# A looped general path behind the main code, a split first exponential and a separate last tile, in an attention kernel

## The chip, the core and the metric

The kernel runs on one core of a Trainium2 chip. The metric is device time in microseconds (us) of one execution. The profile describes one execution each. Engines are PE (TensorE, matmuls; PEld its weight loads), ACT (ScalarE, here the exponentials), DVE (VectorE), POOL (GpSimd) and SP (SyncE, here issuing most transfers); "PEq" and the like are their sequencers.

## The reference

```python
B, Hq, Hkv, Sq, Sk, D = 16, 32, 8, 288, 512, 128       # bf16
k = jnp.repeat(k, Hq // Hkv, axis=1); v = jnp.repeat(v, Hq // Hkv, axis=1)
scores = jnp.einsum("bhqd,bhkd->bhqk", q, k) * D ** -0.5
out = jnp.einsum("bhqk,bhkd->bhqd", softmax(scores), v)
```

There are 16 x 8 = 128 groups (one key/value head with its four query heads: 1152 query rows, nine tiles of 128). The kernel leaves out the subtraction of the row maximum. Every row sum of exponentials is checked against a range; if one falls outside, a **general path** at the end computes everything again with the maximum. With the inputs given it never runs, but its code is part of the program.

## The kernel before

A group is three chunks of 1536 score columns (NC = 3, 384 chunks in all). For each chunk PE makes six score matmuls (`op_s`), ACT one exponential (`op_exp`), PE twelve matmuls with the values (`op_pv`, two chunks later, LAG = 2), DVE a reciprocal and a scaling. Where the general path stands, and how the end chooses it:

```python
def general(eng, key, after):                # called in each engine's head
    home[key] = nc.cur_bb
    br = eng.br(after + key)                 # jump over the general path ...
    if key in hints:
        br.branch_hint(hints[key])           # ... hinted at an earlier place
    with nc.body("general_" + key):
        ...
        fns[key](eng)                        # its unrolled code
        eng.br("done_" + key)
    nc.switch_bb(after + key)

def choose(eng, key, behind=False):          # at each engine's end
    eng.wait_ge(sem["s_flag"], 1)
    reg = eng.alloc_register("bad_" + key)
    eng.load(reg, flag_i[:])
    ...
    br = eng.br_ne(reg, 0, "general_" + key, "done_" + key)
    ...                                      # PE alone has its general path here
```

The heads of ACT, PE and SP:

```python
@block.scalar
def _(eng):
    op_kd(eng, 0)                            # load of key group 0, 128 KB
    ...
    emit(eng, [("s_one", 1)], lambda: eng.activation(dum[:, 1:2], dum[:, 0:1], ACTF.Exp))
    op_kc(eng, 0, range(NJ // 2, NJ), 1, 2)  # copy of half the transposed keys
    op_kd(eng, 1)                            # key group 1, 128 KB
    op_v(0, eng, 0, 2)                       # values of groups 0 and 1, 256 KB
    general(eng, "act", "main_")
    for n in range(NS):
        op_exp(n)
    op_ev_act()                              # scales the very last query tile
    choose(eng, "act")

@block.tensor
def _(eng):
    for x in range(WARM): ...                # 5 matmuls of zeros, 512 columns
    op_kt(0, range(half), 0)                 # key transposes
    op_kt(0, range(half, NJ), 1)
    for n in range(NS):
        if n == LAG:
            op_kt(1, range(NJ), 1)
        ...
        op_s(n)
        if n >= LAG:
            op_pv(n - LAG)
    ...

first = [lambda i=i: op_q0(i) for i in range(NC)]   # SP: query group 0 in 3 parts
first += [lambda: op_q(1), lambda: op_k(0, 2), lambda: op_q(2), ...]
```

Of the kernel before, what the change touches and what calls it, by code (L numbers as in the profile page):

```python
# [16 lines left out]
def general_path(nc, es, q, k, v, out, s_go):  # L17

    B, Hq, Sq, D = q.shape
    _, Hkv, Sk, _ = k.shape  # L20
    rep = Hq // Hkv
    P = 128
    NJ = Sk // P
    NT = (rep * Sq) // P
    G = Hkv
    NG = B * G
    U = NG * NT
    UPB = G * NT
    FREE = NJ * P
    scale = float(D) ** -0.5  # L30
    DV = D + 1
    OPB = 3
    NSB, NXB, NS, NX, NPB, NM, NR, XPB = 3, 3, 3, 4, 4, 8, 2, 2
    LAG_XT, LAG_PV = 3.0, 8.0
    n_xc = U // XPB
    n_oc = U // OPB

    q_v = q.rearrange("b h s d -> b (h s) d")
    k_v = k.rearrange("b g s d -> b (g s) d")
    o_v = out.rearrange("b h s d -> b (h s) d").rearrange("b (c p) d -> b p c d", p=P)  # L40
    v_v = v.rearrange("b g s d -> b (g s) d").rearrange("b (c p) d -> b p c d", p=P)

    v_sb = es.enter_context(nc.sbuf_tensor("gv_sb", [P, 2, G, NJ, DV], BF16))
    o_sb = es.enter_context(nc.sbuf_tensor("go_sb", [P, 2, G, NT, D], BF16))
    qt_sb = es.enter_context(nc.sbuf_tensor("gqt_sb", [P, 2, G, NT, P], BF16))
    kt_sb = es.enter_context(nc.sbuf_tensor("gkt_sb", [P, 2, G, NJ, P], BF16))
    sn_sb = es.enter_context(nc.sbuf_tensor("gsn_sb", [P, NS, FREE], FP32))
    x_sb = es.enter_context(nc.sbuf_tensor("gx_sb", [P, NX, FREE], BF16))
    pt_sb = es.enter_context(nc.sbuf_tensor("gpt_sb", [P, NPB, XPB, NJ, P], BF16))
    nmx_sb = es.enter_context(nc.sbuf_tensor("gnmx_sb", [P, NM], FP32))  # L50
    rl_sb = es.enter_context(nc.sbuf_tensor("grl_sb", [P, NR, OPB], FP32))
    ident = es.enter_context(nc.sbuf_tensor("gident", [P, P], BF16))
    ones_sb = es.enter_context(nc.sbuf_tensor("gones_sb", [P, P], BF16))
    ps_s = es.enter_context(nc.psum_tensor("gps_s", [P, NSB, FREE], FP32))
    ps_x = es.enter_context(nc.psum_tensor("gps_x", [P, NXB, XPB, NJ, P], BF16))
    ps_o = es.enter_context(nc.psum_tensor("gps_o", [P, 2, 512], FP32))

    class Chan:
        def __init__(self, name, n):
            self.n = n  # L60
            self.sems = [es.enter_context(nc.semaphore("g_%s%d" % (name, i))) for i in range(n)]

        def w(self, i, mult=1):
            return (self.sems[i % self.n], (i // self.n + 1) * mult)

        def s(self, i):
            return self.sems[i % self.n]

    c_ldq = Chan("ldq", 2)
    c_ldk = Chan("ldk", 2)  # L70
    c_ldv = Chan("ldv", 2)
    c_out = Chan("outd", 2)
    c_s = Chan("s", NSB)
    c_dve = Chan("dve", NS)
    c_pool = Chan("pool", NX)
    c_xt = Chan("xt", NX)
    c_xc = Chan("xc", NXB)
    c_exp = Chan("exp", NPB)
    c_pv = Chan("pv", 7)
    c_rc = Chan("rc", NR)  # L80
    c_oev = Chan("oev", 2)
    s_init = es.enter_context(nc.semaphore("g_init"))
    s_c0 = es.enter_context(nc.semaphore("g_c0"))

    def emit(eng, waits, fn):
        for (s, n) in waits[:-1]:
            eng.wait_ge(s, n)
        ins = fn()
        if waits:
            s, n = waits[-1]  # L90
            ins.wait_op(s, n, "sem-ge")
        return ins

    def op_load(b):
        eng = nc.sync
        bb = b % 2
        if b >= 2:
            last = (b - 1) * UPB - 1
            eng.wait_ge(*c_s.w(last))
            eng.wait_ge(*c_pv.w(last))  # L100
            eng.wait_ge(*c_xt.w(last))
        eng.dma_start_transpose(
            qt_sb[:, bb].rearrange("d g t p -> d (g t p)"), q_v[b]).then_inc(c_ldq.s(b), 16)
        eng.wait_ge(*c_ldq.w(b, 16))
        eng.dma_start_transpose(
            kt_sb[:, bb].rearrange("d g j p -> d (g j p)"), k_v[b]).then_inc(c_ldk.s(b), 16)
        eng.wait_ge(*c_ldk.w(b, 16))
        eng.dma_start(
            v_sb[:, bb].rearrange("p g j e -> p (g j) e")[:, :, 0:D], v_v[b]).then_inc(c_ldv.s(b), 16)
        eng.wait_ge(*c_ldv.w(b, 16))  # L110

    def op_store(b):
        eng = nc.sync
        r = (b + 1) * UPB // OPB - 1
        eng.wait_ge(*c_oev.w(r))
        eng.wait_ge(*c_oev.w(r - 1))
        eng.dma_start(
            o_v[b], o_sb[:, b % 2].rearrange("p g t d -> p (g t) d")).then_inc(c_out.s(b), 16)
        eng.wait_ge(*c_out.w(b, 16))

    def op_s(u):
        eng = nc.tensor
        g, t = u // NT, u % NT
        bb, gl = (g // G) % 2, g % G
        waits = []
        if u % UPB == 0:
            waits += [c_ldq.w(g // G, 16), c_ldk.w(g // G, 16)]
        if u >= NSB:
            waits.append(c_dve.w(u - NSB))
        emit(eng, waits, lambda: eng.matmul(  # L130
            ps_s[:, u % NSB, :], qt_sb[:, bb, gl, t, :],
            kt_sb[:, bb, gl].rearrange("p j c -> p (j c)"), start=True, stop=True)
        ).then_inc(c_s.s(u), 1)

    def op_dve(u):
        eng = nc.vector
        waits = []
        if u >= NS:
            waits.append(c_pool.w(u - NS))
        waits.append(c_s.w(u))  # L140
        emit(eng, waits, lambda: eng.tensor_scalar(
            out=sn_sb[:, u % NS, :], in0=ps_s[:, u % NSB, :],
            scalar1=-scale, scalar2=None, op0=ALU.mult, op1=ALU.min,
            accum_out=nmx_sb[:, u % NM:u % NM + 1])
        ).then_inc(c_dve.s(u), 1)

    def op_pool(u):
        eng = nc.gpsimd
        waits = []
        if u >= NX:  # L150
            waits.append(c_xt.w(u - NX))
        waits.append(c_dve.w(u))
        emit(eng, waits, lambda: eng.tensor_scalar(
            out=x_sb[:, u % NX, :], in0=sn_sb[:, u % NS, :],
            scalar1=-1.0, scalar2=nmx_sb[:, u % NM:u % NM + 1],
            op0=ALU.mult, op1=ALU.add)
        ).then_inc(c_pool.s(u), 1)

    def op_xt(u):
        eng = nc.tensor  # L160
        c, slot = u // XPB, u % XPB
        waits = []
        if slot == 0 and c >= NXB:
            waits.append(c_exp.w(c - NXB))
        waits.append(c_pool.w(u))
        ins = None
        for j in range(NJ):
            ins = emit(eng, waits if j == 0 else [], lambda: eng.transpose(
                ps_x[:, c % NXB, slot, j, :], x_sb[:, u % NX, j * P:(j + 1) * P], ident[:]))
        ins.then_inc(c_xt.s(u), 1)  # L170

    def op_exp(c):
        eng = nc.scalar
        waits = []
        if c >= NPB:
            waits.append(c_pv.w((c - NPB) * XPB + 1))
        waits.append(c_xt.w(c * XPB))
        waits.append(c_xt.w(c * XPB + 1))
        emit(eng, waits, lambda: eng.activation(
            pt_sb[:, c % NPB].rearrange("p a j c -> p (a j c)"),  # L180
            ps_x[:, c % NXB].rearrange("p a j c -> p (a j c)"),
            ACTF.Exp)
        ).then_inc(c_exp.s(c), 1)

    def op_pv(u):
        eng = nc.tensor
        g = u // NT
        bb, gl = (g // G) % 2, g % G
        c, slot = u // XPB, u % XPB
        r, oslot = u // OPB, u % OPB  # L190
        waits = []
        if u % UPB == 0:
            waits.append(c_ldv.w(g // G, 16))
        if oslot == 0 and r >= 2:
            waits.append(c_oev.w(r - 2))
        if slot == 0:
            waits.append(c_exp.w(c))
        ins = None
        for j in range(NJ):
            ins = emit(eng, waits if j == 0 else [], lambda: eng.matmul(  # L200
                ps_o[:, r % 2, oslot * DV:(oslot + 1) * DV],
                pt_sb[:, c % NPB, slot, j, :], v_sb[:, bb, gl, j, :],
                start=(j == 0), stop=(j == NJ - 1)))
        ins.then_inc(c_pv.s(u), 1)

    def op_rc(r):
        eng = nc.vector
        waits = []
        if r >= NR:
            waits.append(c_oev.w(r - NR))  # L210
        waits.append(c_pv.w(r * OPB + OPB - 1))
        src = ps_o[:, r % 2, 0:OPB * DV].rearrange("p (a e) -> p a e", e=DV)[:, :, D:DV]
        emit(eng, waits, lambda: eng.reciprocal(
            rl_sb[:, r % NR, :], src.rearrange("p a e -> p (a e)"))
        ).then_inc(c_rc.s(r), 1)

    def op_oev(r):
# [35 lines left out]
    def run(key):  # L253
        for (_, _, fn) in sched[key]:
            fn()
# [538 lines left out]
```

## Time and profile before

| | |
|---|---|
| time, median of 3 runs | 531.61 us (531.57 to 532.08) |
| span of the profiled run | 530.00 us (1.72 less than that run's time) |
| head: fourth exponential (number 3) ends | 15.40 us |
| steady stage: to the last whole exponential's end | 509.22 us |
| tail: last exponential's end to the end of the span | 3.98 us |

The steady stage is 379 exponentials, 1.343 us apart. The rows that carry head and tail stand in the prediction. I use "exponential 3" as the end of the head, as from there on exponentials run back to back. One view more is needed later, the window of PE's clock ahead of the first clock record. (Two clock records of this trace last 3.41 us each, full clock from 7.17 and half, 0.50, from 10.58; a "window" is below such a stretch, and the one ahead of a first record is counted back from it. Columns: stretch, length, busy time of PE, PEld, DVE, ACT and POOL with counts, granted clock, DMA share, GB/s.)

```profile
3.76:7.17 3.41, 2.85 (x16) 1.68 (x14) 0.29 (x1) 0.38 (x1) 0.00 (x0) 1.00 0.69 180
```

PE was busy for 2.85 of 3.41 us here, and full clock is on record from 7.17. The clock column's 1.00 is no record of this window: the trace's first one starts at 7.17, and the first chunk's six matmuls took 1.44 us (4.56 to 6.00) against 0.82 for a later chunk (the one that starts at 14.53). The warm matmuls of 512 columns follow each other at 0.42 to 0.43 us, 0.83 ns a column, against 0.43 ns in the steady stage (0.66 us for a chunk's 1536 columns in the chain), so I take PE to be at half clock until then.

### The profile page before, as it was taken

Reading aid. Unit: us, or ns where it says so; the run is one execution under the profiler, and the core shown is the slowest. Engines: PE = TensorE matmul, PEld = TensorE weight load, DVE = VectorE, ACT = ScalarE, POOL = GpSimd, SP = SyncE. Lnnn points to the kernel's source line nnn. Section 1 sums busy time; section 2 is a strip of 40 time slices with the busy share of each in tenths; the row PEclk is TensorE's granted clock in tenths of the full one; section 3 lists DMA queues with packets and bytes.
Section 4 is the critical chain, followed back from the end, with each engine's and each line's share of the span. In section 5 each row is a group of like instructions: output and inputs, shape, how many; then the busy total and the mean of one; then the engine's idle time right before and its main releaser. Section 6 shows DMA issues by size and latency. Waiting matters only on the chain.

```text
span 530.0 us, 16353 instructions
## 1 busy us (share of the span) xinstructions
PE 522.2 (99%) x6927; PEld 457.3 (86%) x6927; DVE 289.5 (55%) x812; ACT 518.4 (98%) x389; POOL 74.2 (14%) x135
## 2 busy tenths in 40 slices
PE   6999999999999999999999999999999999999997
PEld 4888888888888888888888888888888888888886
DVE  1555555555555555555555555555555555555555
ACT  4999999999999999999999999999999999999997
POOL 1211011111110111111111011101111101111000
PEclk8999999999999999999999999999999999999999
DMA  8999999899999999999999999999989998997112
GB/s 158 232 201 260 211 217 252 190 211 232 226 261 186 237 211 240 203 232 246 233 206 211 225 195 213 275 190 208 249 200 245 201 207 202 216 213 192 68 69 90
DMA packets 253150, 110.17 MB, mean 208 GB/s; under 512 B 219792, under 2 KB 236816, under 8 KB 253072
## 3 DMA queue, kind: packets, MB, share of 16 engines
q1 hardware_dynamic: 252512, 108.56, 97.0%
q8 instruction: 55, 0.90, 0.7%
q10 hardware_dynamic: 560, 0.52, 0.3%
q14 instruction: 23, 0.19, 0.2%
HBM read 17.04 MB, written 37.75 MB: 103 GB/s over the span
## 4 chain that ended last, share of the span: by engine, by line
PE 98%; issue 0%; ACT 0%; DVE 0%; DVEq 0%
PE ps_o L557 49%; PE ps_s L536 48%; PE ps_o L683 0%; ACT pt_sb L586 0%; PE ps_s L568 0%; PE ps_o L516 0%; DVE o_sb L623 0%; ACT kt_sb L524 0%; DVE z_sb L734 0%; PE ps_o L700 0%; DVE bad_sb L649 0%; DVE rl_sb L603 0%; DVE flag_i L761 0%; DVE bad_sb L646 0%; DVEq L737 0%
## 5 line engine op out<-in xcount | busy, mean ns | idle before, releaser
L586 ACT ACTIVATE pt_sb<-ps_s 128x1536 bf16<-128x1536 f32 x385 | 516.2, 1738 | 5.4 <-issue 4.3
L557 PE MATMUL ps_o<-v_sb,pt_sb 128*128 128x129 bf16 x4596 | 323.8, 220 | 0.0
L536 PE MATMUL ps_s<-qt_sb,kt_sb 128*128 128x384 bf16 (+2 forms) x2304 | 319.2, 275 | 3.3 <-ACT pt_sb L586 2.7
L557 PEld LDWEIGHTS ps_o<-v_sb,pt_sb 128*128 128x128 bf16 x4596 | 292.7, 98 | 25.0 <-issue 0.3
L613 DVE TENSOR_TENSOR o_sb<-ps_o,rl_sb 128x384 bf16<-128x384 f32 x383 | 213.5, 558 | 13.5 <-DVE rl_sb L603 0.2
L536 PEld LDWEIGHTS ps_s<-qt_sb,kt_sb 128*128 128x128 bf16 x2304 | 180.0, 98 | 41.0 <-ACT pt_sb L586 2.9
L603 DVE RECIPROCAL rl_sb<-ps_o 128x3 f32<-128x3 f32 x383 | 69.3, 181 | 217.5 <-PE ps_o L557 217.5
L596 POOL COPY v_sb<-vd_sb 128x512 bf16<-128x512 bf16 x128 | 73.3, 617 | 413.5 <-DMA vd_sb<-in_v_dram 308.8
L524 DVE COPY kt_sb<-ps_o 128x256 bf16<-128x256 bf16 (+1 forms) x2 | 0.7, 358 | 6.0 <-PE ps_o L516 6.0
L683 PE MATMUL ps_o<-z_sb 128*128 128x512 bf16 x5 | 2.3, 629 | 1.3 <-DVE z_sb L734 1.3
L639 DVE TENSOR_REDUCE st_sb<-rl_sb 128x1 f32<-128x72 f32 (+1 forms) x16 | 3.5, 216 | 0.0
L641 DVE TENSOR_REDUCE st_sb<-rl_sb 128x1 f32<-128x72 f32 (+1 forms) x16 | 3.5, 216 | 0.0
L709 ACT ACT_TABLE_LOAD x1 | 1.3, 1283 | 1.3 <-PEq L779 1.3
L683 PEld LDWEIGHTS ps_o<-z_sb 128*128 128x128 bf16 x5 | 0.6, 134 | 2.1 <-DVE z_sb L734 1.3
L524 ACT ACTIVATE kt_sb<-ps_o 128x256 bf16<-128x256 bf16 x1 | 0.4, 384 | 1.2 <-PE ps_o L516 1.2
L516 PEld LDWEIGHTS ps_o<-ident,kd_sb 128*128 128x128 bf16 x8 | 0.8, 127 | 0.8 <-DMA kd_sb<-in_k_dram 0.6
L700 PE MATMUL ps_o<-bad_sb,one_f 128*1 128x25 f32 x2 | 0.2, 184 | 1.0 <-DVE bad_sb L649 1.0
L700 PEld LDWEIGHTS ps_o<-bad_sb,one_f 128*1 128x1 f32 x2 | 0.1, 80 | 1.2 <-DVE bad_sb L649 1.2
L516 PE MATMUL ps_o<-ident,kd_sb 128*128 128x128 bf16 x8 | 1.1, 273 | 0.0
L630 ACT ACTIVATE o_sb<-ps_s,rl_sb 128x128 bf16<-128x128 f32 x1 | 0.4, 368 | 0.7 <-DVE rl_sb L603 0.7
L568 PE MATMUL ps_s<-v_sb,pt_sb 128*128 128x129 bf16 x12 | 0.9, 222 | 0.0
L568 PEld LDWEIGHTS ps_s<-v_sb,pt_sb 128*128 128x128 bf16 x12 | 0.7, 98 | 0.2 <-ACT pt_sb L586 0.2
(20 smaller groups left out, 3.6 us busy)
## 6 DMA issues: line engine op xcount, KB each, us to landing
out_dram<-o_sb SPq DMA_DIRECT2D x127, 288.0 KB, 4.1
vd_sb<-in_v_dram SPq DMA_DIRECT2D x31, 512.0 KB, 5.5
qt_sb<-in_q_dram SPq DMA_TRANSPOSE x130, 5.0
kt_sb<-in_k_dram SPq DMA_TRANSPOSE x32, 5.2
out_dram<-o_sb SPq DMA_DIRECT2D x3, 96.0 KB, 1.6
kd_sb<-in_k_dram ACTq DMA_DIRECT2D x2, 128.0 KB, 2.5
vd_sb<-in_v_dram ACTq DMA_DIRECT2D x1, 256.0 KB, 3.7
vd_sb<-in_v_dram SPq DMA_DIRECT2D x1, 256.0 KB, 4.5
```

The lines of the kernel that those rows point to most:

```text
L516: ins = emit(eng, [("s_id", 2), ("s_kd%d" % g, 16)], lambda: eng.transpose(dst[:, x * P:(x + 1) * P], kd_sb[:, g, j * D:(j + 1) * D], iden ...
L536: ins = emit(eng, waits if x == 0 else [], lambda: eng.matmul(ps_s[:, n % 2, c:c + w], kt_sb[:, sl, j, gi, :], qg[:, r0:r0 + w], start=Tru ...
L557: ins = emit(eng, waits if a == 0 and j == 0 else [], lambda: eng.matmul(outs(r)[:, a, :], pt_sb[:, r % NPT, j, a * P:(a + 1) * P], v_sb[: ...
L568: ins = emit(eng, [("s_e", NS + (0 if a < TPC - 1 else 1))], lambda: eng.matmul(outs(NS - 1)[:, a, :], pt_sb[:, (NS - 1) % NPT, j, a * P:( ...
L586: emit(eng, waits, lambda: eng.activation(d, s, ACTF.Exp, scale=scale)).then_inc(sem["s_e"], 1)
L596: emit(eng, waits, lambda: eng.tensor_copy(v_sb[:, sl, gi * NJ:(gi + 1) * NJ, 0:D], vd_sb[:, sl, gi].rearrange("p (j d) -> p j d", d=D))). ...
L603: emit(eng, [("s_pv", r + 1)], lambda: eng.reciprocal(rl_sb[:, TPC * r:TPC * (r + 1)].unsqueeze(2), outs(r)[:, :, D:DV])).then_inc(sem["s_ ...
L613: emit(eng, waits, lambda: eng.tensor_tensor(out=o_sb[:, g % NO, t0:t0 + TPC, :], in0=outs(r)[:, :, 0:D], in1=rl_sb[:, TPC * r:TPC * (r + ...
L639: emit(eng, [("s_rc", e // TPC)], lambda: eng.tensor_reduce(st_sb[:, 0, b:b + 1], rl_sb[:, a:e], AX.X, ALU.max))
L641: eng.tensor_reduce(st_sb[:, 1, b:b + 1], rl_sb[:, a:e], AX.X, ALU.min).then_inc(sem["s_stat"], 1)
L683: emit(eng, [("s_z", 1)], lambda: eng.matmul(ps_o[:, 1, :], z_sb[:, 0:P], z_sb[:], start=True, stop=True))
L709: emit(eng, [("s_one", 1)], lambda: eng.activation(dum[:, 1:2], dum[:, 0:1], ACTF.Exp))
```

## The change

Its aim is to take the long unrolled general path out of the engines' heads and to polish both ends. (1) The general path is rewritten as a small loop and stands behind the main code on every engine; the four jumps over it go. (2) The key copy goes from ACT to DVE, so ACT's queue issues the value load and key group 1 at once instead of behind the wait for that copy. (3) The first exponential is cut after 512 columns. (4) Ten small warm matmuls are added. (5) The last query tile is scaled by DVE and stored alone. (6) The two range checks no longer wait for each other.

```diff
-        def general(eng, key, after): ...
-        def choose(eng, key, behind=False):
+        def choose(eng, key):
             ...
+            eng.br_ne(reg, 0, "general_" + key, "done_" + key)
+            with nc.body("general_" + key):
+                ...
+                fns[key](eng)              # loops over 128 groups x 9 tiles
+                eng.br("done_" + key)
+            nc.switch_bb("done_" + key)
 ...
         def op_exp(n):
+            if n == 0:
+                d, s = parts[0]
+                emit(eng, [("s_s0", 1)], lambda: eng.activation(d[:, 0:BANK], s[:, 0:BANK], ACTF.Exp, scale=scale))
+                parts = [(d[:, BANK:CH], s[:, BANK:CH])]
 ...
         @block.tensor
+            op_warm(WARM, BANK, ps_o[:, 1])
+            op_kt(0, range(NJ), 0)
+            op_warm(6, P, ps_s[:, 1])
             for n in range(NS):
                 if n == LAG:
                     op_kt(1, range(NJ), 1)
+                    op_warm(4, P, ps_o[:, 0])
 ...
         @block.scalar
-            op_kc(eng, 0, range(NJ // 2, NJ), 1, 2)
+            op_v(0, eng, 0, 2)
             op_kd(eng, 1)
-            op_v(0, eng, 0, 2)
-            general(eng, "act", "main_")
             for n in range(NS):
                 op_exp(n)
-            op_ev_act()
 ...
         def op_ev_last():                  # DVE: two tiles, then the last one
+            emit(eng, [("s_pl", 1)], lambda: eng.reciprocal(
+                rl_sb[:, c + n:c + TPC], src[:, n, D:DV])).then_inc(sem["s_rc"], 1)
+            emit(eng, [("s_rc", NS + 1)], lambda: eng.tensor_scalar(
+                out=dst[:, n, :], in0=src[:, n, 0:D], scalar1=rl_sb[:, c + n:c + TPC], ...
 ...
         def op_over(hi, lo, x0, x1, wait):
-            emit(eng, [("s_stat", n)], lambda: eng.scalar_tensor_tensor(
+            eng.tensor_scalar(
```

## The prediction

> **What bounds the kernel now.** I read the page's head first, then its chain of waits, then the exponential's instructions in two windows, and last the head and the tail in order of time.
>
> ```profile
> PE 522.2 (99%) x6927; PEld 457.3 (86%) x6927; DVE 289.5 (55%) x812; ACT 518.4 (98%) x389; POOL 74.2 (14%) x135
> PE 98%; issue 0%; ACT 0%; DVE 0%; DVEq 0%
> ```
>
> Two engines look full, and the chain names PE. The windows of the exponential (line 586) decide between them:
>
> ```profile
> L586 ACT ACTIVATE pt_sb<-ps_s x38: 1444/1582/1736, 13.9 to 63.5; 128x1536 bf16<-128x1536 f32 x38
> L586 ACT ACTIVATE pt_sb<-ps_s x299: 1762/1762/1763, 98.4 to 498.7; 128x1536 bf16<-128x1536 f32 x150
> ```
>
> An exponential of 1536 columns lasts 1444 ns when it finds ACT free, and 1762 ns later, growing in between: a backlog. In the trace the early starts are 1335 ns apart (PE's pace) and the ends 1343 ns apart. The 8 ns difference piles up over 40 steps, until PE must wait for the exponential two steps back; from then on starts are 1343 to 1344 ns apart as well. So **ACT bounds the steady stage**, with PE under 1% behind it. The main loop has 384 steps: 382 x 1.343 = 513 us lie there, and the change touches none of it. What can move is the head (until exponentials run back to back) and the tail.
>
> The head, from the timeline of ACT, PE and PEld:
>
> ```profile
> 4.42 0.55 ACTq L460 DMA_DIRECT2D vd_sb<-in_v_dram  x1
> 4.56 2.72 PE L536 MATMUL ps_s<-qt_sb,kt_sb 128*128 128x384 bf16 x12 [0.56 <-ACT kt_sb L524]
> 8.70 4.13 ACT L586 ACTIVATE pt_sb<-ps_s 128x1536 bf16<-128x1536 f32 x3 [4.28 <-issue]
> 10.20 0.65 PEld L536 LDWEIGHTS ps_s<-qt_sb,kt_sb 128*128 128x128 bf16 x6 [2.86 <-ACT pt_sb L586]
> 13.95 4.23 ACT L586 ACTIVATE pt_sb<-ps_s 128x1536 bf16<-128x1536 f32 x3 [1.12 <-PE ps_s L536]
> ```
>
> The first score chunk is complete at 6.00 us (last matmul's end in the trace), the second at 7.28, but the first exponential starts at 8.70 after 4.28 us of "issue": it waited for no semaphore. ACT's own records show why: a compare-and-branch at 5.00 to 5.05 us (the jump over the unrolled general path), then nothing for 3.65 us. PE is meanwhile without work for 2.7 us, and the windows show the price:
>
> ```profile
> 7.00:10.50 3.50, 0.81 (x8) 0.50 (x7) 0.42 (x1) 1.80 (x2) 1.17 (x2) 1.00 1.26 175
> 10.50:14.00 3.50, 3.50 (x27) 2.78 (x25) 0.74 (x2) 2.38 (x3) 0.00 (x0) 0.51 1.33 198
> ```
>
> (first the stretch, its length and PE's busy time; third from the end the granted clock). After an idle window PE runs a whole window at 0.51 of its clock, the fourth exponential comes late, and ACT idles 1.12 us. The fourth exponential ends at 15.40; back-to-back work runs from there to the last whole one's end at 524.62.
>
> The tail: the last half exponential ends at 526.02.
>
> ```profile
> 525.67 1.91 SPq L500 DMA_DIRECT2D out_dram<-o_sb  x3
> 527.76 0.17 DVE L761 TENSOR_REDUCE flag_i<-ps_o 1x1 int32<-1x25 f32 x1 [0.30 <-PE ps_o L700]
> L334 SPq DRAIN  x1: 136/136/136, 529.4 to 529.4; - x1
> L334 DVEq DRAIN  x1: 141/141/141, 529.6 to 529.6; - x1
> ```
>
> The last store is issued at 527.25 and its landing is seen by SP at 528.89; the flag is ready at 527.93, loaded by 528.5. Then come branches: ACT and POOL go on within 0.04 us, SP takes 0.41, PE's branch itself 0.50, and DVE 1.02 until its drain at 529.64. The span ends 0.23 us after that drain, at 530.00. The time (531.61) is 1.6 us more than the span.
>
> [...] The trace shows one window of 3.41 us at half. [...] For 1536 columns [...] this trace has 1444 to 1451 and 1343, so I use 171 ns fixed.
>
> **The change part by part.** 1. *General path behind the main code.* Removes four taken branches from the head. SP's gap (12.02 to 12.55) shrinks, DVE and POOL had slack, ACT gains its 3.65 us stall, as far as its inputs allow.
>
> 2. *Key copies.* ACT loses its copy of half the transposed keys (0.38 us), DVE copies all four tiles after the fourth transpose (ends 4.00) in the 0.42 us that such a 512-column copy takes at 7.55: 4.04 to 4.46, against ACT's end at 4.42. The scores start 0.04 us later: chunk 0 ends at 6.04, chunk 1 at 7.32.
>
> 3. *Exponential in two parts.* 512 columns after the second matmul (5.19): 171 + 427 = 0.60 us, to 5.82. The rest after 6.04: 6.08 + 0.171 + 0.853 = 7.10. In one part: 6.08 + 1.45 = 7.53. But exponential 1 needs chunk 1 at 7.32 and could start behind the unsplit one at about 7.44 (ends 8.87) against 7.36 (ends 8.81). So the split is worth under 0.1 us, and I expect that even this is lost at step 5.
>
> 4. *Ten small warm matmuls.* Six fill the wait for the key copy (4.00 to 4.46, free); four of 55 ns precede chunk 2, at 7.35 to 7.6: 0.2 us on PE, hidden, as ACT is busy to 8.81.
>
> 5. *What then binds.* Chunk 2 ends about 8.4, exponential 2 at 8.81 + 1.34 = 10.15. Chunk 3 needs query group 1: that transposed load is issued at 4.93 by SP and lands at 9.30 in the trace, and nothing in the change moves it. Chunk 3: 9.30 + 0.04 + 0.83 = 10.17, exponential 3: 10.21 + 1.45 = 11.66, against 11.49 if ACT never idled. The other inputs are in time: value groups 0 and 1 are issued about 1.7 us earlier, key groups 2 and 3 land at 11.80 and query group 2 at 12.72, needed at about 13.4; group 3 at 15.89, needed at 17.4; group 4 at 20.97, needed at 21.4 (0.4 us to spare). PE now idles under half a microsecond at a time, so the window at half clock should go.
>
> Head's sum: exponential 3 ends at 11.66 instead of 15.40, **3.74 us**; the old one lost another 0.1 at exponential 4 (its end is 1.44 us later, not 1.34). I take 3.8. The 379 steps after it are ACT's 1.3433 us each: the last whole exponential ends at 520.8, the last part 1.41 later at 522.2.
>
> 6. *Tail.* Old: 526.02 to 530.00, 3.98 us. In old times: the first two tiles' sums are complete at 526.22, but DVE is busy with the evacuation before until 526.41. Reciprocal 0.18, scaling of 256 columns 0.43, to about 527.06; one more reciprocal and a scaling of 128 columns on DVE (from 558 and 425 ns for 384 and 256 columns: about 0.29), to 527.48. Store of the last tile at 527.56 instead of 527.25, landing 1.6 later at 529.2: **0.3 us later**. The unchained checks save one wait of some 0.04 us and one semaphore, start later by 0.3, and give the flag at about 528.16, off the path, as its load ends at 528.7. In return [...] the general path is now some tens of instructions: SP's 0.41 and DVE's 1.02 shrink to some 0.05. SP: 529.2 + 0.1 + drain 0.14 + 0.23 to the end = 529.7. Net gain **0.3 us**.
>
> Sum: 3.8 + 0.3 = 4.1 us; 531.6 - 4.1 = 527.5.
>
> **The rivals.** *A: the start stall only moves* [...]. [...] Against: POOL and PE, running straight on, show no such gap. It would leave 530 to 531.6. *B: query group 1 binds harder or not at all.* If the earlier value load pushes it by 0.5 us, 528.0; if it lands 0.2 earlier, 527.3. *C: PE becomes the bound or goes cold in another window.* Half clock over one window costs up to 1.7 us of PE work, of which ACT's queue hides little that early: 529. Against: busy windows from 3.7 on. *D: the tail's longer DVE chain is not paid back* [...]: 0.3 lost instead of 0.3 gained, 528.1. *E: the steady pace changes.* Same instructions on ACT; each 1 ns a step would be 0.4 us.
>
> **Range and chances.** The centre is 527.5; B and D pull to either side by some 0.5, A in part and C to 529 or more. An 80% range is 526.3 to 529.3. For 2% the kernel would have to lose 10.6 us; head and tail outside the loop hold about 12 altogether, so faster by over 2% is nearly excluded; slower would take 28 ns on every exponential, which nothing adds.
>
> **What would show each step.** The first ACTIVATE of line 586's successor at about 5.2 us with 512 columns, without "issue" before it; exponential 3 ending near 11.7, with chunk 3 released by the query load; no window at half clock between 7 and 20 us; 1343 ns between later exponentials; the last exponential near 522.2; the last store about 1.6 us after it and drains within 0.2 us of SP's last branch. I am wrong if ACT still shows "issue" before its first exponential, if the half-clock window stays, or if steady steps differ by more than 2 ns.

Some figures need a word. Step 3's 427 and 853 ns, and the 171 ns fixed, used a rate per column; the profile after bears them out, with 597, 1023 and 1450 ns for 512, 1024 and 1536 columns, that is 0.833 ns a column and 171 ns besides. The 0.09 us by which exponential 1 starts ahead of the other's end (7.44 against 7.53) has no source; the trace before has 0.11, 1.45 us each and 1.34 apart. The 55 ns of a small warm matmul (step 4) fit the chain before, 0.68 us for twelve value matmuls of 129 columns. Rival C's 1.7 us are half of the 3.41 us at half clock. That SP's 0.41 and DVE's 1.02 us would shrink to some 0.05, and that the window at half clock would go, were estimates; the profile before does not show either.

## The result, and the profile after

The changed kernel takes **529.28 us** (median of four runs, 528.53 to 529.86); the kernel before took 531.85 (531.57 to 533.25). The ratio is 0.9946, interval 0.9923 to 0.9968: about half a per cent faster. Ratios here and below are the mean time of one kernel's fast runs over that of the other's of the same rounds, so not quite the ratio of the medians quoted. The result lies inside the predicted range, at its upper edge, 1.8 us above the centre.

The page of the changed kernel: totals, chain, and the row of the whole exponentials (busy, mean ns, idle before, what ended it).

```profile
PE 522.6 (99%) x6937; PEld 457.8 (87%) x6937; DVE 289.9 (55%) x814; ACT 518.0 (98%) x388; POOL 74.0 (14%) x135
...
PE 98%; DMA 1%; DVE 1%; issue 0%
...
L417 ACT ACTIVATE pt_sb<-ps_s 128x1536 bf16<-128x1536 f32 (+1 forms) x385 | 515.9, 1738 | 1.2 <-PE ps_s L361 1.2
```

Two things are to be seen. The bound is the same. And ACT's idle time before the exponentials of line 417 (all but the first part of the first one) is now 1.2 us in all and ends on PE, with no "issue". What replaced it is the DMA in the chain; the timeline of the head shows where (start, length, engine, line, operation, idle time before it and what ended that):

```profile
1.29 0.39 ACTq L280 DMA_DIRECT2D vd_sb<-in_v_dram  x1
1.71 0.54 ACTq L261 DMA_DIRECT2D kd_sb<-in_k_dram  x1
5.81 2.74 PE L361 MATMUL ps_s<-qt_sb,kt_sb 128*128 128x384 bf16 x12 [0.58 <-DMA qt_sb<-in_q_dram]
6.46 0.60 ACT L411 ACTIVATE pt_sb<-ps_s 128x512 bf16<-128x512 f32 x1 [3.73 <-PE ps_s L361]
8.77 0.63 PE L349 MATMUL ps_o<-z_sb 128*128 128x128 bf16 x4
9.20 1.49 PE L361 MATMUL ps_s<-qt_sb,kt_sb 128*128 128x384 bf16 x6
10.72 4.23 ACT L417 ACTIVATE pt_sb<-ps_s 128x1536 bf16<-128x1536 f32 x3 [0.68 <-PE ps_s L361]
```

The value load is issued at 1.29 instead of 4.42. The first scores, which waited for the key copy before, now wait for the *query* transfer and start at 5.81 instead of 4.56: its first part landed at 5.76 (3.72 before). They then take 2.74 us for two chunks, and the next chunk 1.49, against 0.82 for the one from 11.30: that is half clock, which the windows confirm.

```profile
3.93:7.35 3.42, 2.79 (x17) 1.93 (x18) 0.42 (x1) 0.64 (x2) 1.16 (x2) 1.00 1.01 201
7.35:10.76 3.41, 3.41 (x23) 2.62 (x22) 0.42 (x1) 2.47 (x3) 0.00 (x0) 1.00 1.15 204
10.76:14.00 3.24, 3.24 (x49) 2.94 (x47) 1.48 (x4) 3.24 (x3) 1.17 (x2) 1.00 1.17 203
```

In this run the first clock record, full, starts only at 10.76: PE does 23 instructions in the window before it and 49 in the shorter one after. The steady stage takes 509.12 us, as before but for a loss of 0.10 us at its first step that is gone. The tail, and the last drains of the engines (of a line's view: durations in ns, then the start):

```profile
523.79 2.11 SPq L320 DMA_DIRECT2D out_dram<-o_sb  x4
...
526.03 0.20 DVE L578 TENSOR_REDUCE flag_i<-ps_o 1x1 int32<-1x50 f32 x1 [0.34 <-PE ps_o L525]
```

```profile
L170 DVEq DRAIN  x1: 17/17/17, 527.1 to 527.1; - x1
...
L170 SPq DRAIN  x1: 7/7/7, 527.7 to 527.7; - x1
```

DVE's branch ends at 526.91 and its drain starts at 527.07, 0.16 later (1.02 before); SP needs 0.13 (0.41 before). The books of the two profiled runs close:

| us | before | after | gain |
|---|---|---|---|
| exponential 3 ends | 15.40 | 13.61 | 1.79 |
| to the last whole exponential | 509.22 | 509.12 | 0.10 |
| tail, from the last exponential's end | 3.98 | 3.78 | 0.20 |
| time less span | 1.72 | 1.94 | -0.22 |
| time of that run | 531.72 | 529.86 | 1.86 |

(The 1.41 us from the last whole exponential's end to the last part's are the same in both.) So the question is why the head gave 1.79 us and not the 3.74 predicted.

### The profile page after: what moved, and what is told of

It is laid out like the page before. It is cut to its first block, busy times and chain, and to the rows that moved or that the text cites. A ratio compares the mean times of both kernels' runs of the same rounds, so it can differ in the third digit from the quotient of the medians.

```text
span 527.9 us, 16369 instructions
## 1 busy us (share of the span) xinstructions
PE 522.6 (99%) x6937; PEld 457.8 (87%) x6937; DVE 289.9 (55%) x814; ACT 518.0 (98%) x388; POOL 74.0 (14%) x135
## 4 chain that ended last, share of the span: by engine, by line
PE 98%; DMA 1%; DVE 1%; issue 0%
PE ps_o L384 49%; PE ps_s L361 49%; DMA qt_sb<-in_q_dram 1%; DVE o_sb L445 0%; DVE rl_sb L435 0%; PE ps_o L349 0%; PE ps_o L336 0%; DVE o_sb L456 0%; DVE o_sb L461 0%; PE ps_o L525 0%; DVE flag_i L578 0%; DVE bad_sb L479 0%; DVE bad_sb L477 0%; DVE rl_sb L459 0%
## 5 line engine op out<-in xcount | busy, mean ns | idle before, releaser
L417 ACT ACTIVATE pt_sb<-ps_s 128x1536 bf16<-128x1536 f32 (+1 forms) x385 | 515.9, 1738 | 1.2 <-PE ps_s L361 1.2
L349 PE MATMUL ps_o<-z_sb 128*128 128x512 bf16 (+1 forms) x9 | 2.9, 487 | 1.3 <-DVE z_sb L553 1.3
```

What stands on the lines that cost most here:

```text
L349: emit(nc.tensor, [("s_z", 1)], lambda: nc.tensor.matmul(dst[:, 0:w], z_sb[:, 0:P], z_sb[:, 0:w], start=True, stop=True))
L417: emit(eng, waits, lambda: eng.activation(d, s, ACTF.Exp, scale=scale)).then_inc(sem["s_e"], 1)
```

## The experiments

Three theories stood against each other. **Interference and clock:** the value load and key group 1, issued early, share the DMA engines with the first query transfer and delay it (from 0.8 to 6 us the packets of ACT's queue took 53.1% of the time of the 16 engines in the kernel after, 14.5% in the kernel before, beside 31.2% and 25.1% of SP's); PE then waits for it, and runs another window of 3.41 us at half clock. **Added PE work:** the ten warm matmuls, four of them ahead of chunk 2, cost the time. **Another bound:** the head can't end much before 13 us, wherever the general path stands. "Late" and "early" below are always about the two loads on ACT. All twelve experiments gave correct results. Here they are in one table with the two kernels; each is discussed below. Landings, clock, exponential 3 and tail are those of one profiled run each; "full clock from" is the start of its first record of full clock.

| kernel | median us | ratio to before | first query part lands | full clock from | exponential 3 ends | tail |
|---|---|---|---|---|---|---|
| before | 531.61 | 1 | 3.72 | 7.17, half again 10.58 to 14.00 | 15.40 | 3.98 |
| after | 529.28 | 0.9946 | 5.76 | 10.76 | 13.61 | 3.78 |
| after_again | 528.34 | 0.9916 | 5.43 | 9.47 | 12.81 | 3.78 |
| late_loads | 528.33 | 0.9920 | 3.48 | 7.10 | 11.96 | 3.78 |
| v_late | 528.03 | 0.9914 | 4.71 | 7.18 | 11.86 | 3.78 |
| k_late | 529.26 | 0.9935 | 5.39 | 4.29 | 12.90 | 3.78 |
| no_warm4 | 529.10 | 0.9932 | 5.40 | 10.08 | 12.87 | 3.78 |
| warm14 | 527.73 | 0.9906 | 5.29 | 4.72 | 11.48 | 3.78 |
| before_early | 530.29 | 0.9955 | 5.17 | 12.93 | 14.64 | 3.98 |
| place_only | 527.67 | 0.9908 | 3.49 | 6.58 | 12.06 | 3.61 |
| place_split | 527.45 | 0.9902 | 3.50 | 7.07 | 11.74 | 3.61 |
| place_two | 528.28 | 0.9917 | 3.53 | 7.30 | 12.32 | 3.61 |
| place_tail | 528.33 | 0.9916 | 3.50 | 6.65 | 12.07 | 3.78 |
| unrolled_behind | 531.36 | 0.9972 | 3.47 | 6.70 | 12.07 | 7.00 |

Medians are of different calls, whose kernel before varied from 531.85 to 533.20 in its median; ratios compare across calls, but their intervals are about 0.002 to 0.003 to either side, 1 us and more, so most neighbours in the table overlap (the kernel before alone spread from 530.3 to 534.3 us in these calls, which ran on two chips). The columns of the profile separate what the ratios can't.

### late_loads: the two loads held until the first query part is in

```diff
# of the kernel after
+            for (s, n) in need(eng, [("s_qp0", 16)]):
+                eng.wait_ge(s, n)
             op_v(0, eng, 0, 2)
             op_kd(eng, 1)
```

> The changed kernel, but ACT waits for the first part of query group 0 to land before it issues the loads of value groups 0, 1 and key group 1. Theory T1 (these loads, issued at 1.3 and 1.7 us instead of 4.4 and 4.0, share the DMA engines with the first query part and key group 0 and delay them): the first query part lands near 3.7 to 4.0 us instead of 5.76, key group 0 near 3.2 instead of 3.93, score chunk 0 starts near 4.6 instead of 5.81, exponential 3 ends near 11.7 instead of 13.6, time 527.3 to 528.0. Rival T2 (the landing of 5.76 was chance, or PE's slow clock to 10.65 us was the cause): chunk 0 starts anywhere, the time stays at 528.5 to 529.9.

The first query part landed at 3.48, chunk 0 started at 4.62, full clock came at 7.10 and exponential 3 ended at 11.96: 1.65 us earlier than in the kernel after (0.85 earlier than in its repeat below).

```profile
4.62 2.66 PE L361 MATMUL ps_s<-qt_sb,kt_sb 128*128 128x384 bf16 x12
...
9.17 4.13 ACT L417 ACTIVATE pt_sb<-ps_s 128x1536 bf16<-128x1536 f32 x3 [0.40 <-PE ps_s L361]
```

The 0.40 us are a wait that this kernel adds: key group 1, held back too, landed at 7.82 (6.13 in the kernel after), and chunk 2 stands behind its transposes. The ratio is 0.9920 (0.9901 to 0.9939); the median of 528.33 lies between the two expectations. The profiled run, the slowest of six (529.32, the rest 528.17 to 528.50), lost about 1.1 us again later, on a query load that came late at step 15:

```profile
26.89 0.82 PE L361 MATMUL ps_s<-qt_sb,kt_sb 128*128 128x384 bf16 x6 [1.05 <-DMA qt_sb<-in_q_dram]
27.74 5.48 ACT L417 ACTIVATE pt_sb<-ps_s 128x1536 bf16<-128x1536 f32 x4 [1.00 <-PE ps_s L361]
```

So the profile shows the earlier landing and the earlier head, but the time doesn't: the repeat of the kernel after has the same median (528.34), and its three fastest runs (527.48 to 527.89) are faster than any run here. And the ladder of query loads behind the head has little slack: in this run one late transfer took 1.1 us back.

### place_only: nothing but the place of the general path

```diff
# of the kernel before
-general_path(...)                 # unrolled; jumped over in each head
+general_path(...)                 # the looped one of the kernel after
-            general(eng, "act", "main_")        # and on SP, DVE, POOL
-            choose(eng, "pe", behind=True)
+            choose(eng, "pe")     # choose() of the kernel after: path behind main code
```

> The kernel before with the looped general path behind the main code and nothing else. T1: loads as before (query part at 3.7, chunk 0 at 4.6), no stall of ACT, exponential 3 ends near 11.7, the last drain right after SP's last branch: 527.4 to 528.2, which is better than the whole change. T2: head and clock as in the changed kernel, 529 to 530. Rival A of the prediction (the stall only moves): 530.5 to 531.6.

527.67 us (527.52 to 527.95 in six runs), ratio 0.9908 (0.9889 to 0.9927). One part of the change alone gives all that the whole change gave, and its median is 1.6 us lower (0.7 lower than that of the repeat below). Its head's timeline:

```profile
4.45 0.45 ACTq L279 DMA_DIRECT2D vd_sb<-in_v_dram  x1
6.05 4.13 ACT L405 ACTIVATE pt_sb<-ps_s 128x1536 bf16<-128x1536 f32 x3 [1.62 <-PE ps_s L355]
9.06 0.85 PE L376 MATMUL ps_o<-v_sb,pt_sb 128*128 128x129 bf16 x12 [0.67 <-POOL v_sb L415]
10.61 2.79 ACT L405 ACTIVATE pt_sb<-ps_s 128x1536 bf16<-128x1536 f32 x2 [0.42 <-PE ps_s L355]
```

The first exponential starts when its scores are there (6.05) and no longer at 8.70, so the stall was the jump, and nothing took its place. Then 0.42 us are lost at exponential 3: the first value matmuls wait for POOL's copy of the values, which landed at 8.34, and chunk 3 stands behind them in PE's order. The theory of another bound near 13 us falls: the head can end at 12.06 with the old loads (11.7 was expected).

### unrolled_behind: the old, unrolled general path at the new place

The diff is that of place_only without the new general path.

> The kernel before with its own large unrolled general path moved behind the main code: position without size. If the head's gain is of position alone, exponential 3 ends near 12.0 as with the small one; the jump to the end then passes thousands of instructions, so drains come 0.4 to 1.0 us after the branches and the tail is 4.0 to 4.6 us after the last exponential instead of 3.61: 528.0 to 528.7. If size matters at the start too, exponential 3 ends later than 13.

The head is that of place_only to 0.02 us. But the time is 531.36 us (ratio 0.9972, 0.9949 to 0.9996), far from the 528.0 to 528.7 expected, as the tail takes 7.00 us instead of 3.61 (4.0 to 4.6 expected). The branches and drains at the end, by their lines' views:

```profile
L372 ACTq COMPARE_BRANCH  x1: 50/50/50, 525.0 to 525.0; - x1
...
L372 PEldq COMPARE_BRANCH  x1: 4137/4137/4137, 525.1 to 525.1; - x1
```

```profile
...
L334 ACTq DRAIN  x1: 80/80/80, 528.4 to 528.4; - x1
...
L334 PEldq DRAIN  x1: 68/68/68, 529.3 to 529.3; - x1
```

Here the jump goes over the long code at the end: PE's branch alone lasts 4.14 us, ACT's next record is 3.3 us behind its branch. So the **place** of the path buys the head, and its **size**, at that place, buys the tail. The place without the small size gives 0.3%; a small path at the old place was not run.

### no_warm4: without the four warm matmuls ahead of chunk 2

```diff
# of the kernel after
-                    op_warm(4, P, ps_o[:, 0])
```

> The changed kernel without the four warm matmuls ahead of chunk 2. If they cost what the trace shows (8.77 to 9.20 us at half clock, PE being what chunk 2 waits for), chunk 2 ends about 0.4 us earlier and the time falls by 0.3 to 0.4. Rival (they raise the clock earlier): the full clock comes a window (3.4 us) later and the time rises by up to 1.5 us.

Exponential 3 ended at 12.87, 0.74 earlier than in the first profile of the kernel after, but within 0.06 of its second (12.81); the ratios, 0.9932 (0.9906 to 0.9957) and those of the kernel after, overlap. At half clock the four stand on PE's path with 0.43 us, the step of 107 ns from one to the next; that is all that the added work can claim, and with the first query part at 5.40 and full clock only from 10.08 the head stays near 13 us. It is no rival for the bulk.

### before_early: the early loads alone, in the kernel before

```diff
# of the kernel before
-            op_kc(eng, 0, range(NJ // 2, NJ), 1, 2)
-            op_kd(eng, 1)
             op_v(0, eng, 0, 2)
+            op_kd(eng, 1)
+            op_kc(eng, 0, range(NJ // 2, NJ), 1, 2)
```

> The kernel before with the loads of value groups 0, 1 and key group 1 issued ahead of ACT's key copy, at 1.3 to 2.2 us. T1: the first query part lands near 5.8, chunk 0 starts near 5.8 instead of 4.56; ACT's stall to 8.4 to 8.7 us hides most of it, PE idles less, so the time is 530.3 to 531.9. T2: chunk 0 still starts near 4.6.

The first query part landed at 5.17 instead of 3.72, so the delay comes with the loads' order alone. The time still fell, to 530.29 (ratio 0.9955, 0.9929 to 0.9980), as the timeline explains:

```profile
5.21 2.74 PE L536 MATMUL ps_s<-qt_sb,kt_sb 128*128 128x384 bf16 x12 [1.11 <-DMA qt_sb<-in_q_dram]
7.70 2.79 ACT L586 ACTIVATE pt_sb<-ps_s 128x1536 bf16<-128x1536 f32 x2 [3.17 <-issue]
```

ACT reaches its jump earlier (the branch ends at 4.20), so the stall, 3.5 us long here too, ends a microsecond sooner. Half clock lasted until 12.93 (chunk 2, from 9.20 on, took 1.46 us).

### v_late and k_late: one load held at a time

```diff
# v_late, of the kernel after
+            op_kd(eng, 1)
+            (wait for s_qp0, as in late_loads)
             op_v(0, eng, 0, 2)
-            op_kd(eng, 1)
# k_late, of the kernel after
             op_v(0, eng, 0, 2)
+            (wait for s_qp0, as in late_loads)
             op_kd(eng, 1)
```

> The changed kernel with only the 256 KB value load held back until the first query part has landed; key group 1 (128 KB) stays early, at 1.3 us. T1a (both loads crowd the first ones, by bytes): the query part lands between 3.5 and 5.4, nearer 4.2. T1b (the value load alone is to blame): near 3.5, as with both held back. Time between 528.0 and 528.8.

> The changed kernel with only key group 1's 128 KB load held back; the 256 KB value load stays early, at 1.3 us. T1a: the query part lands near 4.8. T1b: near 5.4 to 5.8, as in the changed kernel. Time 528.6 to 529.4.

With the keys early and the values held, the first query part landed at 4.71; with the values early and the keys held, at 5.39, about as late as with both. So the 256 KB of values do most of the harm, the 128 KB of keys less. The two delays (1.9 and 1.2 us against late_loads) don't add up to that of both together (2.0 to 2.3). v_late ended exponential 3 at 11.86 (ratio 0.9914, 0.9883 to 0.9945). k_late brings a new wait: key group 1 landed at 8.75, and chunk 2's way through the transposes with it, so exponential 3 ended at 12.90 although full clock came early, at 4.29.

### after_again: the kernel after, unchanged

> The changed kernel once more, beside the others on one chip: 528.5 to 529.9; query part landing at 5.0 to 6.0 us, exponential 3 ending at 12.8 to 13.8, tail 3.78 us after the last exponential. If the landing of 5.76 was chance, it is 3.5 to 4.0 here.

528.34 us, ratio 0.9916 (0.9890 to 0.9941). The six runs fall in two clusters, 527.48 to 527.89 (three) and 528.79 to 529.18 (three); the four of the first call, 528.53 to 529.86, go with the upper one. In the profiled one (529.06) the query part landed 0.33 us earlier than in the first profile, full clock came 1.29 us earlier (9.47), and exponential 3 ended 0.80 earlier. So the very same program spreads over 2.4 us, and a comparison with it must use both sets of runs. The record has the spans of the other runs too: 525.5 to 526.0 us in the lower cluster. With the 509.12, 1.41 and 3.78 us that the rest takes in both of its profiles, exponential 3 ended there at about 11.2 to 11.7 (an estimate), where warm14 below has it.

### warm14: late query kept, PE's idle time filled

```diff
# of the kernel after
-            op_warm(6, P, ps_s[:, 1])
+            op_warm(14, P, ps_s[:, 1])
```

> The changed kernel with 14 instead of 6 small warm matmuls ahead of chunk 0, so that PE is busy until the late query part has landed. If PE's idle 0.6 to 0.8 us there is what keeps the clock at half for another window, the full clock comes by 7.5 us, exponential 3 ends by 12.5 though chunk 0 starts at 5.4 to 5.8 as before, and the time is 527.6 to 528.4. If the landing alone decides, or the window's phase, exponential 3 stays at 12.8 to 13.6 and the runs spread from 527.5 to 529.9 as before.

If it is the clock that costs, filling the wait for the query part must bring the gain although the part stays late. It landed at 5.29, and:

```profile
3.90 1.34 PE L349 MATMUL ps_s<-z_sb 128*128 128x128 bf16 x14
5.34 1.48 PE L361 MATMUL ps_s<-qt_sb,kt_sb 128*128 128x384 bf16 x12
6.26 5.22 ACT L417 ACTIVATE pt_sb<-ps_s 128x1024 bf16<-128x1024 f32 x4
...
9.18 0.82 PE L361 MATMUL ps_s<-qt_sb,kt_sb 128*128 128x384 bf16 x6 [0.33 <-DMA qt_sb<-in_q_dram]
```

Two chunks took 1.48 us instead of 2.74, ACT ran without a gap, and exponential 3 ended at 11.48, the earliest of all kernels. The ratio is 0.9906 (0.9888 to 0.9924), with five runs within 0.6 us (527.43 to 528.02) and no second cluster. In this profile full clock is on record already from 4.72, after a window (1.31 to 4.72) in which PE was busy throughout. The filling has little part in that: six small matmuls from 3.90 would have kept PE busy up to 4.54, so for all but 0.2 us of the window (an estimate). The profile therefore shows that an early full clock makes up for a late query part: with both, the head ended 0.48 us before that of late_loads, which had the part at 3.48 and full clock from 7.10. It doesn't show what the late part costs at a clock that comes at 7 us, and that the filling brings the early clock in every run is suggested by the missing second cluster only.

### place_two, place_split, place_tail: one part each on top of place_only

place_two loads query group 0 in two transfers instead of three, so that query group 1 is issued earlier:

```diff
# of place_only
-            c0, c1 = i * TPC, (i + 1) * TPC
+            c0, c1 = ((0, TPC), (TPC, NT))[i]
-        first = [lambda i=i: op_q0(i) for i in range(NC)]
+        first = [lambda i=i: op_q0(i) for i in range(2)]
```

> The placement-only kernel (small general path behind, nothing else) with query group 0 loaded in two transposes (3 and 6 tiles) instead of three. The prediction's step 5 (query group 1 binds the head next, by SP's issue time of 1.25 us a transpose): query group 1 is issued at 3.6 instead of 4.9 and lands near 8.1 to 8.4, ACT's wait before exponential 3 (0.42 us) goes, exponential 3 ends at 11.5 to 11.7 instead of 12.06: 527.1 to 527.4, the fastest of all. Rival: the landing does not follow the issue (the DMA engines are the limit) and it stays at 527.5 to 527.9.

The time was 528.28 us, ratio 0.9917 (0.9901 to 0.9933). The idea failed: query group 1 did land earlier, at 7.84 instead of 9.40, but exponential 3 ended later, at 12.32, as the values landed at 8.61 (8.34) and in that kernel it is they that bind:

```profile
9.32 0.85 PE L376 MATMUL ps_o<-v_sb,pt_sb 128*128 128x129 bf16 x12 [0.92 <-POOL v_sb L415]
```

place_split adds the split exponential alone (the lines of `op_exp` and its semaphore in the diff above):

> The placement-only kernel with the first exponential in two parts and nothing else. As query group 1 binds exponential 3, the split is worth nothing: exponential 0 ends 0.4 us earlier, exponential 3 still ends at 11.9 to 12.1, 527.5 to 527.9. Rival (the split helps as intended): exponential 3 ends 0.3 to 0.4 us earlier.

527.45 us (527.21 to 527.91), ratio 0.9902 (0.9881 to 0.9923): not to be told from place_only. The first exponential ended at 7.07 instead of 7.50, exponential 1 at 8.74 instead of 8.84, so 0.1 us reached it. The 0.32 us by which exponential 3 is earlier than in place_only equal the earlier landing of the values, 8.02 against 8.34; the split moves no load, and the landing differs from run to run.

place_tail adds the new tail and range checks alone (`op_ev_last`, the fourth store, `op_over`):

> The placement-only kernel with the new tail (last tile scaled and stored by itself on DVE, checks unchained) and nothing else. From the profiles: 3.78 us from the last exponential's end to the span's end instead of 3.61, last store issued 1.41 us after it instead of 1.23: 0.17 us slower, 527.7 to 528.1. Rival (the new tail is a gain): 3.5 us or less.

528.33 us (528.06 to 528.43), against 527.45 for place_split. Head and last exponential are place_only's to 0.01 us; the last store is issued 1.41 us after the last exponential instead of 1.23, as the scaling of the last tile on DVE waits for the one before it:

```profile
523.10 0.42 DVE L445 TENSOR_TENSOR o_sb<-ps_s,rl_sb 128x256 bf16<-128x256 f32 x1
523.44 0.16 DVE L448 RECIPROCAL rl_sb<-ps_s 128x1 f32<-128x1 f32 x1
523.63 0.35 DVE L450 TENSOR_SCALAR o_sb<-ps_s,rl_sb 128x128 bf16<-128x128 f32 x1
```

So the tail is 3.78 instead of 3.61. Besides, the time exceeds the span by 1.94 us, against 1.69. That holds in every profiled run: 1.94 in all eight with the new tail, 1.69 to 1.78 in all six with the old. What lies outside the span no view shows; it stays open.

## Why the prediction was right or wrong

**The bound and the steady stage (first part, rival E): right.** From exponential 3 to the last whole one every profile has 509.12 us, but for the kernel before (509.22) and late_loads (510.22, the late query load).

**Step 1, the stall goes: right.** Rival A, the stall that moves, is out: in place_only and in the kernel after, the first exponential waits for PE's scores and nothing else. The half-clock window behind the stall (0.50 from 10.58 to 14.00, after a window with 0.72 us of PE work) is gone too. One argument against A was none, though: POOL doesn't run straight on, it jumps as well (its branch stands at 1.13 in the kernel before), and its next work waited for a load until 8.20, so it could show no gap.

**Step 3, the split is worth under 0.1 us: right** (0.10 at exponential 1, nothing to be told in the time).

**Step 5 failed, in the sentence "The other inputs are in time: value groups 0 and 1 are issued about 1.7 us earlier".** I counted the value load as a benefit and left the query part of group 0 at its old landing, with chunk 0 at about 4.6. It was issued 3.1 us earlier in fact (1.29 against 4.42): ACT's queue no longer waits for the key copy and issues it while the table load (1.23 to 2.51) still runs. There it meets the first query transfer, which is under way from 0.82. The profile counts the packets of both queues on the same 16 DMA engines: from 0.8 to 6 us those of ACT's queue took 53.1% of their time, 14.5% before. The landing is 3.47 to 3.72 in all seven profiles with both loads late, 4.71 with only the keys early, and 5.17 to 5.76 in all six with the values early. My rival B thought of this for query group 1 only; that one landed at 9.11 (9.30 before), about as predicted, and did not bind in the kernel after.

**What the late landing did was mostly through the clock, and here rival C came true.** The prediction took full clock from about 7 us on. Here the first record of full clock lies anywhere from 4.29 to 12.93, and for the very same program at 10.76 and 9.47. In the profiles the window ahead of the first record was busy for 2.84 or 2.85 us in six kernels with the loads late (in late_loads all 3.41) and full clock followed. With the wait for the query part in it, the kernel after reached 2.79 us (3.93 to 7.35), the repeat 2.72, no_warm4 2.65 and before_early 2.60, and half clock stayed for one window more. The other two with the values early, warm14 and k_late (3.02), had a window that closed before the wait weighed on it. The gap between 2.79 and 2.84 is thin (PE idles 0.56 us in that window in the kernel before, too, against 0.63), and these are modelled times, so this is a pattern over the profiles, not a measured edge; late_loads and v_late (3.31) lie well clear of it. That PE's wait is what kept the clock at half is my reading of this pattern; no run shows it alone. In the kernel after, chunks 0 and 1 took 2.74 us, hardly more than in the kernel before (2.72), but began 1.25 us later, and chunk 2 took 1.49 us where one at full clock takes 0.82; exponentials 1, 2 and the first one's second part waited for PE, 1.2 us in all.

**The mis-sized term is the head: 3.74 us predicted, 1.79 measured** (2.59 in the repeat). How the missing 1.95 divides is an estimate, for a clock that rises at about 7 us, as the prediction had it. In the kernel after the first exponential ended at 8.33; with full clock from 7.35, chunk 1 would be done by about 8.0, later chunks soon enough, and exponentials 1 to 3 would follow back to back, to 8.33 + 3 x 1.343 = 12.36. So about 0.7 us of the miss (12.36 against 11.66) is the late landing itself, and 1.25 (13.61 against 12.36) the further window at half clock, in which the four warm matmuls of step 4, "0.2 us on PE, hidden", count 0.43 us on PE's path. That the two clusters of the kernel after (527.5 and 529) are the position of the window is the likely reading, since nothing else in the two profiles differs as much; but both profiles are of the upper cluster, and only they show where full clock begins, so it is argued and not shown. That the result still fell in the predicted range is no merit of the centre: the range reached to 529.3 for rivals A and C, and C's price was paid.

**Step 5's own bound was there where the clock let it through.** In warm14 chunk 3 waited 0.33 us for query group 1 (9.18), as the step said, but ACT had work until then, and the head ended at 11.48, where the prediction has "11.49 if ACT never idled".

**Step 6, the tail: both halves right in sign, the sum not.** The new tail alone costs 0.17 us (3.78 against 3.61; 0.3 predicted) and the shorter branches give 0.37 (3.98 against 3.61; 0.6 predicted): 0.20 net inside the span. But the 0.22 us that the time lies further above the span take it back. (The prediction's 1.6 us for that distance set the time of other runs against the profiled run's span; it is 1.72.) So rival D's "not paid back" is nearer than my "net gain 0.3". The range checks are off the path, as said: the flag is ready at 526.23, and SP's branch, which waits for the last store, ends at 527.57.

The lowest medians are those of place_split, place_only and warm14 (527.45 to 527.73); the lower cluster of the kernel after reaches them. The head of warm14 with the old tail would combine the best parts (about 0.4 us less than warm14, by 0.17 of tail and 0.25 outside the span, an estimate); it was not run.

## What to carry to other kernels

A jump over the long code cost ACT 3.3 to 3.65 us here, at the start as at the end: put rarely used code behind the main code, and make it small, and check both ends. A load that is moved to an earlier place is not free because its issue is (here 384 KB put off the first query part by 1.4 to 2.3 us, before_early against before, after against late_loads): ask which transfer at that moment the first compute waits for, and compare landings before and after. Ahead of full clock, half a microsecond of idle time may go with a whole further window at half speed, as in the kernel after, where PE idled 0.63 us from 3.93 to 7.35 and ran at half clock until 10.76 (in the kernel before, a window with 0.56 us of idle time was followed by full clock); matmuls of zeros that fill the gap are worth a try, though the one profile of it here owes most to the window's position.
